# Spreading the last 224 maxima of an attention kernel over 68 units, making the last half's rows by quarters, and giving half chains banks of their own

## The chip, the cores and the metric

The kernel runs on one core of one Trainium2 chip. Time is device microseconds of one execution, lower is better; a time shown is the median of several runs. Profiles are of one execution each. Engines are called PE (TensorE), PEld (its weight loads), DVE (VectorE), ACT (ScalarE), POOL (GpSimd) and SP (SyncE, which issues most DMAs).

## The reference, cut to what matters

For x of 2048 rows and 512 columns two results are mixed by a gate per row. One is the real part of a two-dimensional Fourier transform, written as matrix products; the other is softmax attention with 32 heads of 16 columns.

```python
a = einsum("bsd,ed->bse", x, hid_re);  b = einsum("bsd,ed->bse", x, hid_im)
A = einsum("ts,bse->bte", seq_re, a) - einsum("ts,bse->bte", seq_im, b)
q, k, v = split_heads(x @ wqkv)                      # 32 heads of 16
B = softmax(q @ k.T / 4) @ v                         # each head 2048 x 2048
y = g * A + (1 - g) * (merge(B) @ wo)                # g = sigmoid(x . gate_w)
```

All of it is float32. The kernel gets its precision by splitting each operand into a rounded high part and a low rest, so that a product is three matmuls (high by high, high by low, low by high).

## The kernel before, in words

**Units.** The heads are taken in 16 pairs p, and a pair's keys in 16 tiles of 128 for each half of the queries. A *unit* u is one key tile for one half (hf) of the queries, so a pair has 32 units and the kernel 512 (`UNITS`). The last 16 units (496 to 511) are cut otherwise: blk 0 (496 to 503) is the first quarter of that half's queries, blk 1 (504 to 511) the second, with two key tiles a unit (L711 to L714).

**Scores and maxima.** The two heads of a pair live in the two halves of PE's rows (h = 0 in rows 0 to 63, h = 1 in rows 64 to 127), so that a matmul of one half can run beside a matmul of the other. `scores` (L707) is one matmul of 50 rows and 512 columns and one exponential on ACT (L722). Rows 48 and 49 of the query stack `qs` hold minus the row maximum, as a high and a low part, so that the exponential's argument is already shifted. Those maxima come from `a_tile` (L216): the same product the other way round, 48 rows, followed by a maximum over 512 columns on DVE (L224). A unit needs four maxima matmuls and eight maxima make one row tile `qt`. When all 64 of a pair's half are there, `m_parts` (a maximum over the rest and a negation on DVE, high and low parts on POOL) and `m_rows` (a transpose on DVE, L241, and eight small DMAs into `qs`, L245: four on SP for h = 0, four on POOL for h = 1) are put into the list `deferred`; one entry of it is taken at the end of each segment. Maxima run ahead of scores by 24 units, so that there are none left for the last 24.

**Values.** For two units together `pv` (L747) multiplies the exponentials with the values, in 16 matmuls of 32 columns into one bank; ACT copies the bank out and POOL adds it to a running sum, which goes to DRAM when a pair's half is done. For the last 16 units `pv_last` (L726) keeps one bank through the eight units of a blk, and `LastPair` (L637) brings its result into the output: `copy`, `turn` (pair sums on PE, reciprocal and product on DVE), `back` (a transpose and a split) and `products` (twelve matmuls of 32 rows, four `finish`es and four output DMAs).

**The rest of PE's work** comes from generators of single matmuls (`Chain`): `real` and `dft` (the Fourier part) and `proj` (the output projection by head groups ct = 0 to 3, three matmuls each). `finish` (L589) adds a chain's bank, times 1 - g, to the output row tile on DVE, or on ACT and POOL for tiles in `by_others`. A matmul of a chain may be cut into the two row halves: half 0 beside scores of h = 1, half 1 beside scores of h = 0.

**Order.** All engine queues are written out by hand. A `segment` (L888) walks a pattern: in each slot it issues one chain half (if the slot has one letter) and one score (s) or maximum (a) of the other row half; a slot of two letters issues one for each row half. At "|" it runs the finishes kept back, the plan and the values of two units. A pair of segments serves four units. THIN goes with the hidden transform, FULL (16 slots) with the long one, NINE (12 and 13 slots, nine chain halves each) with the projection of ct 0 to 2: 14 pairs of NINE, for units 432 to 487. The last 24 units run in the loop at L968: scores of both row halves side by side and whole (128 row) matmuls of `proj` between them (`pump`).

**Plan.** `at` (L817) puts functions on a unit, and `run_plan(u)` runs those for units up to u + 1. Around the end: `sums` at 498 and `inverse` at 500 (the denominators of hf 0, ct 3: a DMA in, a reciprocal on DVE, two DMAs out), `last_block` step 0 at 500 (four loads of `o_raw`, L539 and L540), step 1 (a product), step 2 (a split by `parts`, L562 and L563), `load_w15` at 500 (eight DMAs of the weight rows that `products` needs, L634). For hf 1 step 0 at 486 issues twelve such loads.

**Banks.** Of the eight accumulator banks, `psD` (`d_bank`) belongs to the chains. The other seven rotate: `bank` (L381) takes the one that a small model of DVE and ACT expects to be free first, and `o_bank` takes one of them for a chain or a product.

Of the kernel before, what the change touches and what calls it, by code (L numbers as in the profile page):

```python
# [2 lines left out]

# [6 lines left out]
F32 = mybir.dt.float32  # L10
# [21 lines left out]
def mix_kernel(ctx: ExitStack, tc: tile.TileContext, xa_t, xa, wqkv, w_hid, w_seq, wo, gate_w, out):  # L32
# [183 lines left out]
    def a_tile(i, h, ps=None):  # L216
        p, j = divmod(i, 64)
        qt, kb = divmod(j, 4)
        if ps is None:
            ps = turn_of("a")  # L220
        r = slice(64 * h, 64 * h + 48)
        nc.tensor.matmul(ps, qs[p % 2][r, qt * P:(qt + 1) * P], ks[p % 2][r, kb * 512:(kb + 1) * 512],  # L222
                         start=True, stop=True)
        user = nc.vector.tensor_reduce(mx[p % 2][:, h, qt, kb:kb + 1], ps, AX.X, ALU.max)  # L224
# [6 lines left out]
    def m_parts(p, hf):  # L231

        nc.vector.tensor_reduce(nm[hf].rearrange("p (q h) -> p h q", h=2), mx[p % 2][:, :, 8 * hf:8 * hf + 8, :],
                                AX.X, ALU.max, negate=True)
        t = nhl[hf]
        nc.gpsimd.tensor_copy(t[:, 0], nm[hf])
        nc.gpsimd.tensor_tensor(t[:, 1], nm[hf], t[:, 0].bitcast(F32), ALU.subtract)

    def m_rows(p, hf):

        nc.vector.transpose(mt[hf], nhl[hf].rearrange("p v m -> p (v m)").bitcast(F32))  # L241
        for b in range(4):
            for h in range(2):
                rows = qs[p % 2][64 * h + 48:64 * h + 50, hf * 1024:(hf + 1) * 1024].bitcast(F32)
                (nc.sync, nc.gpsimd)[h].dma_start(rows.rearrange("v (q b c) -> v b q c", q=8, b=4)[:, b],  # L245
                                                  mt[hf][32 * b + h:32 * b + 32:2])

    def run_deferred():
        while deferred:
# [149 lines left out]
    def o_bank():  # L399
# [2 lines left out]
        free[i] = now + 10.0  # L402
        return t

    class Chain:


        def __init__(self, take, n):
            self.take, self.left = take, n
            self.begun = False  # L410

        def mm(self, st, mv, half, stop):
            if not self.begun:
                self.ps = self.take()
            r = slice(None) if half is None else slice(64 * half, 64 * half + 64)
            i = nc.tensor.matmul(self.ps, st[r], mv[r], start=not self.begun, stop=stop)  # L416
            self.begun = True
            return i
# [176 lines left out]
            return  # L595
        nc.vector.scalar_tensor_tensor(y, ps, omg[:, t:t + 1], y, op0=ALU.mult, op1=ALU.add)  # L596

    def proj(hf, cts, pools):

        for qt in range(8):  # L600
            t = hf * 8 + qt
            chain = Chain(pools[qt % len(pools)], 3 * len(cts))
            for ct in cts:
                h1, l1 = oh[hf, ct][qt]
                for i, (st, mv) in enumerate(((h1, 0), (h1, 1), (l1, 0))):
                    last = ct == cts[-1] and i == 2
                    yield chain, st, wos[0][:, mv, ct], partial(proj_next, hf, cts, t, chain) if last else None

    def proj_next(hf, cts, t, chain):
        finish(chain.ps, t, yp[t], t in by_others)  # L610
        if hf == 0 and cts[-1] == 3:
            nc.sync.dma_start(out[t * P:(t + 1) * P, :], yp[t])

    def load_yg(hf, ts):
# [22 lines left out]
    class LastPair:  # L637
# [7 lines left out]
            self.o15 = work.tile([P, 2, P], F32R, name="o15", bufs=2)  # L645

        def copy(self, n):
            for c in range(n):
                cols = slice(c * 512 // n, (c + 1) * 512 // n)
                nc.scalar.copy(self.oe[:, cols], self.acc[:, cols])  # L650

        def turn(self):

# [15 lines left out]
        def products(self, others):  # L669

            pss = [o_bank() for _ in range(4)]
            for i, (st, mv) in enumerate(((0, 0), (0, 1), (1, 0))):
                for c in range(4):
                    r = slice(32 * c, 32 * c + 32)
                    nc.tensor.matmul(pss[c], self.o15[r, st], w15[0][r, mv], start=i == 0, stop=i == 2)  # L675
            for c in range(4):
                t = 8 + 4 * self.blk + c
                y = yp.pop(t)
                finish(pss[c], t, y, c in others)
                nc.sync.dma_start(out[t * P:(t + 1) * P, :], y)  # L680

    last_pairs = []

    def last_pair(fill):
        few.append(work.tile([P, 4, D], F32, name="few", tag="pt", bufs=4))
        x = last_pairs[1]
        x.copy(4)
        by_others.update((5, 6))
        pump(fill, 3)
        pump(fill, 3)  # L690
        x.turn()
        x.back()
        drain(fill)
        x.products((0,))
# [82 lines left out]
    def add_sums():  # L777
        while adds:
            adds.pop(0)()
# [26 lines left out]
    def pump(gen, n):  # L806
        for x in take(gen, n, False):
            issue(x, None)
# [8 lines left out]
    def at(u, f, *args):  # L817
        plan.setdefault(u, []).append(partial(f, *args))
# [11 lines left out]

    for p in range(1, NP):
        at(32 * (p - 1) - 1, load_stacks, p)
    one, more = [d_bank], [d_bank, o_bank, o_bank]
# [18 lines left out]

    FULL = "s a s s a a s s a a s a s a a s |"
    THIN = "aS s a s a s s a s a s a a sA |"
    NINE = "aS s a s a sA a a s a s sA |", "aS a s s a sA a s a s s aS sA |"

    def stream(h):

# [26 lines left out]
            for u in us:  # L885
                pv_last(u)

    def segment(pattern, half, ds, stop):  # L888


        nonlocal now
        nonlocal users
        before, users = users, []
        ds, late = iter(ds), []
        for n, slot in enumerate(pattern.split()):
            if slot == "|":
                for f in late:
                    f()
                add_sums()
                run_plan(valued)  # L900
                values()
                continue
            now += 1
            ahead = pattern == FULL and 0 < n < 15
            if ahead:
                score(slot[0], 1 - half)
            if len(slot) == 1:
                x = next(ds, None)
                if x:

                    before = before if x[0].begun else None
                    i = issue(x, half, stop, late)
# [6 lines left out]
            if not ahead:  # L919
                score(slot[0], 1 - half)  # L920
            if len(slot) == 2:
                score(slot[1].lower(), half)
        if deferred:
            deferred.pop(0)()

    def pairs():

        for i in range(NT - 4):
            yield (THIN,) * 2, take(hid, 12)
        for i in range(2 * NT * 3):  # L930
            yield (FULL,) * 2, take(seq, 16)
        for gen, n in ((proj(1, (0, 1, 2), one), 8), (first, 6)):
            for i in range(n):
                yield NINE, take(gen, 9)

    first = proj(0, (0, 1, 2), one)
    run_plan(0)
    gate()

# [17 lines left out]
            segment(patterns[half], half, ds, half == 1)  # L957


    run_plan(valued)  # L960
    for i in range(4):
        score("s", 1)
    third = proj(1, (3,), more)
    last = proj(0, (3,), more)
    whole = {490: (first, 6), 492: (first, 6), 494: (first, 6), 496: (first, 0),
             498: (third, 6), 500: (third, 6), 502: (third, 6), 504: (third, 3), 506: (third, 3),
             508: (last, 6), 510: (last, 9)}
    for u in range(valued + 2, UNITS, 2):  # L968
        add_sums()
        run_plan(u)  # L970
        for i in range(4):
            if i == 2:
                pump(*whole[u])
                if u == 506:
                    last_pairs[0].turn()
                elif u == 508:
                    last_pairs[0].back()
            for h in range(2):
                scores(u + i // 2, i % 2, h)
            for h in range(2):  # L980
                score("a", h)
        if u == 510:
            last_pairs[0].products(())
        values()
        if deferred:
            deferred.pop(0)()
    assert not any(a_left.values())
    values()
    last_pair(last)


# [34 lines left out]
```

## Time and profile before

| what | before |
|---|---|
| median of 3 runs | 1688.01 us (1687.84 to 1688.89) |
| the profiled execution's own time | 1688.01 us |
| its span | 1686.2 us |
| DVE, ACT, POOL busy | 1370.7, 1246.6, 747.8 us |
| maxima on DVE (L224) | 2022 recorded, mean 683 ns |
| exponentials on ACT (L722) | 2048, mean 629 ns |
| clock granted to PE | 0.999 of full speed |

The page's mean of an instruction is from its start to its end. Neighbours on one engine overlap a little, so the distance between two starts is shorter than the mean and is the number to count with. A busy PE says little, since the ends of matmuls are modelled; the distances between starts say more. A few records of matmuls are missing.

### The profile page before, as it was taken

The page shows a single profiled execution, that of the slowest core. Times are in us where ns is not written, and L with a number is a line of the kernel's source. Part 1 is how long each engine was busy: PE and PEld are TensorE (multiplying, and loading weights), DVE is VectorE, ACT ScalarE, POOL GpSimd, SP SyncE. Part 2 cuts the span into 40 slices and gives each one's busy share as a digit, 9 for nine tenths or more (in the row PEclk, how much of TensorE's full clock was granted, in tenths as well). Part 3 has the DMA queues.
Part 4 walks back from the last instruction along what each step waited for, and adds up shares of the span by engine and source line. Part 5 has one row for each costly group of instructions (what it writes and reads, how often), then busy time and mean ns, then how long its engine had stood idle before and what let it go on. Part 6 is the DMA issues. An engine that isn't in the chain of part 4 may idle for free.

```text
span 1686.2 us, 34488 instructions
## 1 busy us (share of the span) xinstructions
PE 1674.4 (99%) x13072; PEld 1016.5 (60%) x13072; DVE 1370.7 (81%) x2283; ACT 1246.6 (74%) x2472; POOL 747.8 (44%) x807
## 2 busy tenths in 40 slices
PE   9999999999999999999999999999999999999998
PEld 7888766655555555555555555555555555565643
DVE  5448688888888888888888888888888888899944
ACT  5212288887777888777777788778777888787896
POOL 0114634554444465444444466445554465322230
PEclk9999999999999999999999999999999999999999
DMA  9963500314141533314155533332241536740114
GB/s 295 340 151 114 174 10 21 45 51 77 44 83 46 102 97 83 70 46 95 45 132 189 103 121 86 86 68 60 70 89 46 112 96 129 263 70 8 33 27 139
DMA packets 82486, 165.15 MB, mean 98 GB/s; under 512 B 19777, under 2 KB 20033, under 8 KB 78481
## 3 DMA queue, kind: packets, MB, share of 16 engines
q1 hardware_dynamic: 77968, 162.56, 37.3%
q8 instruction: 103, 1.69, 0.5%
q0 software_dynamic: 4352, 0.39, 0.3%
q14 instruction: 63, 0.51, 0.1%
HBM read 107.73 MB, written 54.52 MB: 96 GB/s over the span
## 4 chain that ended last, share of the span: by engine, by line
PE 98%; POOL 1%; DMA 0%; issue 0%; DVE 0%; ACT 0%; DVEq 0%; POOLq 0%; ACTq 0%
PE d L416 38%; PE t L757 27%; PE t L222 12%; PE t L721 8%; PE t L315 4%; PE t L89 2%; PE t L90 2%; PE t L88 2%; PE t L333 1%; PE t L738 1%; PE t L416 0%; DMA raw<-wqkv 0%; POOL hl L292 0%; PE t L675 0%; DMA b<-hl 0%
## 5 line engine op out<-in xcount | busy, mean ns | idle before, releaser
L224 DVE TENSOR_REDUCE mx<-t 128x1 f32<-128x512 f32 x2022 | 1253.9, 683 | 197.6 <-PE t L222 153.1
L722 ACT ACTIVATE pt<-t 128x512 f32<-128x512 f32 x2048 | 1035.1, 629 | 9.5 <-PE t L721 9.3
L721 PE MATMUL t<-qs,ks 50*128 50x512 f32 x2048 | 737.5, 411 | 0.6 <-ACT y L432 0.5
L222 PE MATMUL t<-ks,qs 48*128 48x512 f32 x2022 | 689.9, 400 | 0.0
L416 PE MATMUL d<-xab,ch 64*128 64x512 f32 x2016 | 656.9, 400 | 0.0
L757 PE MATMUL t<-pt,vt 128*32 128x512 f32 x3968 | 477.5, 598 | 0.0
L416 PEld LDWEIGHTS d<-xab,ch 64*128 64x128 f32 x2016 | 357.8, 184 | 132.5 <-issue 99.8
L222 PEld LDWEIGHTS t<-ks,qs 48*128 48x128 f32 x2022 | 366.4, 185 | 91.1 <-ACT pt L722 37.4
L721 PEld LDWEIGHTS t<-qs,ks 50*128 50x128 f32 x2048 | 366.8, 185 | 75.3 <-DVE mx L224 34.9
L416 PE MATMUL d<-xab,cl 64*128 64x512 f32 x1008 | 403.8, 401 | 0.0
L772 POOL TENSOR_TENSOR osum<-osum,oe 128x512 f32<-128x512 f32 x217 | 280.1, 1291 | 164.8 <-ACT oe L766 157.4
L766 ACT COPY oe<-t 128x512 f32<-128x512 f32 x217 | 127.7, 589 | 236.1 <-PE t L757 234.3
L757 PEld LDWEIGHTS t<-pt,vt 128*32 128x32 f32 x3968 | 105.0, 109 | 229.6 <-issue 148.7
L371 POOL CAST ch<-craw 128x512 fp32r<-128x512 f32 x126 | 77.4, 615 | 349.8 <-PE t L721 305.2
L416 PEld LDWEIGHTS d<-xab,cl 64*128 64x128 f32 x1008 | 185.7, 184 | 68.2 <-issue 51.1
L372 POOL TENSOR_TENSOR cl<-craw,ch 128x512 fp32r<-128x512 f32 x126 | 162.6, 1290 | 10.2
L245 POOL DMA_DIRECT2D qs<-mt x128 | 72.3, 570 | 81.9 <-DVE mt L241 75.3
L416 PE MATMUL d<-wo_hl,o_hl 64*128 64x512 f32 (+1 forms) x270 | 72.6, 392 | 0.8 <-DVE yp_qs L596 0.8
L416 PE MATMUL d<-wre,xab 64*128 64x512 f32 x288 | 70.4, 389 | 0.0
L416 PEld LDWEIGHTS d<-wre,xab 64*128 64x128 f32 x288 | 52.9, 185 | 3.8 <-DVE mx L224 0.3
L416 PEld LDWEIGHTS d<-wo_hl,o_hl 64*128 64x128 f32 (+1 forms) x270 | 49.5, 185 | 4.8 <-DVE yp_qs L596 1.3
L89 PE MATMUL t<-xab,wh 128*128 128x512 f32 x128 | 49.9, 390 | 0.2 <-DVE xab L85 0.2
(121 smaller groups left out, 893.3 us busy)
## 6 DMA issues: line engine op xcount, KB each, us to landing
craw<-w_seq SPq DMA_DIRECT2D x128, 256.0 KB
qk<-hl SPq DMA_DIRECT2D x32, 512.0 KB
qs<-qk SPq DMA_DIRECT2D x96, 128.0 KB
ks<-qk SPq DMA_DIRECT2D x96, 128.0 KB
b<-hl SPq DMA_DIRECT2D x16, 512.0 KB
xab<-b SPq DMA_DIRECT2D x16, 512.0 KB
o<-osum SPq DMA_DIRECT2D x62, 128.0 KB
oh<-nh SPq DMA_DIRECT2D x12, 512.0 KB
```

Source lines behind the costliest of these rows:

```text
L89: nc.tensor.matmul(ps, sh, ml, start=False, stop=False)
L222: nc.tensor.matmul(ps, qs[p % 2][r, qt * P:(qt + 1) * P], ks[p % 2][r, kb * 512:(kb + 1) * 512], start=True, stop=True)
L224: user = nc.vector.tensor_reduce(mx[p % 2][:, h, qt, kb:kb + 1], ps, AX.X, ALU.max)
L245: (nc.sync, nc.gpsimd)[h].dma_start(rows.rearrange("v (q b c) -> v b q c", q=8, b=4)[:, b], mt[hf][32 * b + h:32 * b + 32:2])
L371: nc.gpsimd.tensor_copy(h1, raw)
L372: nc.gpsimd.tensor_tensor(l1, raw, h1.bitcast(F32), ALU.subtract)
L416: i = nc.tensor.matmul(self.ps, st[r], mv[r], start=not self.begun, stop=stop)
L721: nc.tensor.matmul(ps, ks[p % 2][rr, kt * P:(kt + 1) * P], qs[p % 2][rr, q0:q0 + 512], start=True, stop=True)
L722: return nc.scalar.activation(pts[u][:, 2 * qb + h], ps, AF.Exp, bias=0.0, scale=DH ** -0.5)
L757: nc.tensor.matmul(acc[32 * j:32 * j + 32], vt[:, kt, p, h:h + 32], pt[:, j], start=u == us[0], stop=u == us[-1])
L766: nc.scalar.copy(oe, acc)
L772: nc.gpsimd.tensor_tensor(o, o, oe, ALU.add)
```

## The change

The 14 NINE pairs and the loop become 20 pairs of segments: 8 of FOURTEEN (14 maxima a pair instead of 16), 3 of NINE, then TEN, TWELVE, TEN, TWELVE, TEN with `proj` of ct 0 to 2, and four pairs with `proj` of ct 3 cut into row halves, of which the first is a TEN and the others have no maxima. The last maximum is now in unit 498's segment. For the second half of pair 15 the rows are made by quarters (n = 4) and not by halves (n = 8), and "^" in a pattern takes one entry of `deferred` in mid-segment. In the four last pairs each row half of a chain is a chain of its own in a bank of its own (`held_bank`), with its own finish. `last_block` of hf 1 moves to 486, 489 and 492, that of hf 0 to 500, 503 and 505 with its product on POOL; `load_w15` stays at 500. The wait of a chain's second half is on the first exponential since the chain's last matmul and not on the last one. The copy of the first `LastPair` goes to DVE; `turn` comes three matmuls earlier in `last_pair`; `products` finishes DVE's tiles first and issues the DMA of ACT's tile from ACT's queue.

```diff
-        hf = j // 32
-        a_left[p, hf] = a_left.get((p, hf), 64) - 1
-        if not a_left[p, hf]:
-            deferred.extend((partial(m_parts, p, hf), partial(m_rows, p, hf)))
+        n = 4 if p == NP - 1 and j >= 32 else 8
+        k = qt // n
+        a_left[p, n, k] = a_left.get((p, n, k), 8 * n) - 1
+        if not a_left[p, n, k]:
+            deferred.extend((partial(m_parts, p, n, k), partial(m_rows, p, n, k)))
...
+    def held_bank():
+
+        i, t = bank()
+        free[i] = 1e9
+        last_held[0] = i
+        return t
...
+        if chain.held is not None:
+            free[chain.held] = now + 5
...
+            copy = nc.scalar.copy if self.blk else nc.vector.tensor_copy
...
+            for c in sorted(range(4), key=lambda c: c not in others):
+                t = 8 + 4 * self.blk + c
+                finish(pss[c], t, yp[t], c in others)
             for c in range(4):
                 t = 8 + 4 * self.blk + c
-                y = yp.pop(t)
-                finish(pss[c], t, y, c in others)
-                nc.sync.dma_start(out[t * P:(t + 1) * P, :], y)
+                (nc.scalar if c in others else nc.sync).dma_start(out[t * P:(t + 1) * P, :], yp.pop(t))
...
         pump(fill, 3)
+        x.turn()
         pump(fill, 3)
-        x.turn()
         x.back()
...
+    last = proj(0, (3,), [o_bank, o_bank, o_bank, o_bank, d_bank, o_bank], range(2, 8))
...
-    for step, u in enumerate((486, 490, 494)):
+    for step, u in enumerate((486, 489, 492)):
         at(u, last_block, step, 1, 3, nc.gpsimd)
-    for step, u in enumerate((500, 506, 506)):
-        at(u, last_block, step, 0, 4, nc.vector)
+    for step, u in enumerate((500, 503, 505)):
+        at(u, last_block, step, 0, 4, nc.gpsimd)
     at(500, load_w15)
...
-    NINE = "aS s a s a sA a a s a s sA |", "aS a s s a sA a s a s s aS sA |"
+    NINE = "aS s a s a ^ sA a a s a s sA |", "aS a s s a ^ sA a s a s s aS sA |"
+    FOURTEEN = "s a s a sS ^ a s s a s a aA |", "aS s a a s ^ s a sS s a s a sA |"
+    TWELVE = ("sA a s a s ^ s a s a s s a s |",) * 2
+    TEN = "aA s s a s ^ s s s a a sS |", "a s a sS a ^ s s s s s aA |"
...
-                            i.ins, dict(before).get("s", before[0][1]).ins.name,
+                            i.ins, dict(before[::-1]).get("s", before[0][1]).ins.name,
...
+        for patterns, n in ((FOURTEEN, 8), (NINE, 3), (TEN, 1), (TWELVE, 1), (TEN, 1), (TWELVE, 1), (TEN, 1)):
             for i in range(n):
-                yield NINE, take(gen, 9)
+                yield patterns, take(both_first, 9)
...
+    after = {504: lambda: last_pairs[0].turn(), 506: lambda: last_pairs[0].back(), 510: in_between}
+    for hf, qts in ((1, range(2)), (1, range(2, 5)), (1, range(5, 8)), (0, range(2))):
+        for half in range(2):
+            ds = take(proj(hf, (3,), [held_bank] * (len(qts) - 1) + one, qts, half == 1), 9, False)
+            if valued < UNITS - 12:
+                pattern = TEN[half]
+            else:
+                pattern = "s s s s s s s s |" if len(qts) < 3 else "s s s s d s s s s |"
+                if valued == UNITS - 2:
+                    pattern = "s s s s d d |"
+            segment(pattern, half, ds, True, after.get(valued), False)
     assert not any(a_left.values())
-    values()
     last_pair(last)
```

`in_between` runs `products` of the first `LastPair` and nine whole matmuls of `last` before the values of unit 510.

More of the change, by code (lines that the diff above doesn't have):

```diff
@@ L2 @@
 from functools import partial
+from itertools import chain as chain_of
 import concourse.bass as bass
@@ L596, in finish, with proj @@
         nc.vector.scalar_tensor_tensor(y, ps, omg[:, t:t + 1], y, op0=ALU.mult, op1=ALU.add)
-    def proj(hf, cts, pools):
-        for qt in range(8):
+    def proj(hf, cts, pools, qts=range(8), whole=True):
+        for n, qt in enumerate(qts):
             t = hf * 8 + qt
-            chain = Chain(pools[qt % len(pools)], 3 * len(cts))
+            chain = Chain(pools[n % len(pools)], 3 * len(cts))
             for ct in cts:
@@ L647, in copy @@
         def copy(self, n):
+            copy = nc.scalar.copy if self.blk else nc.vector.tensor_copy
             for c in range(n):
                 cols = slice(c * 512 // n, (c + 1) * 512 // n)
[L650 removed]
+                copy(self.oe[:, cols], self.acc[:, cols])
         def turn(self):
@@ L886, in values, with segment @@
                 pv_last(u)
-    def segment(pattern, half, ds, stop):
+    def segment(pattern, half, ds, stop, between=None, hold=True):
         nonlocal now
@@ L894, in segment @@
         ds, late = iter(ds), []
+        back = late if hold else None
         for n, slot in enumerate(pattern.split()):
@@ L900, in segment @@
                 run_plan(valued)
+                if between:
+                    between()
                 values()
+                continue
+            if slot == "^":
+                if deferred:
+                    deferred.pop(0)()
                 continue
@@ L911, in segment @@
                     before = before if x[0].begun else None
-                    i = issue(x, half, stop, late)
+                    i = issue(x, half, stop, back)
                     users = []
@@ L915, in segment @@
                         tc.add_manual_dep(
-                            i.ins, dict(before).get("s", before[0][1]).ins.name,
+                            i.ins, dict(before[::-1]).get("s", before[0][1]).ins.name,
                             mybir.DependencyInfo(mybir.DependencyClass.Sync, mybir.DependencyReason.DATA))
                         before = None
-            if not ahead:
+            if not ahead and slot != "d":
                 score(slot[0], 1 - half)
@@ L957, in mix_kernel, with in_between @@
             segment(patterns[half], half, ds, half == 1)
[L960 to L983, printed above, removed]
-        values()
-        if deferred:
-            deferred.pop(0)()
+    def in_between():
+        last_pairs[0].products(())
+        pump(last, 9)
+    after = {504: lambda: last_pairs[0].turn(), 506: lambda: last_pairs[0].back(), 510: in_between}
[9 more added lines that the diff above has]
+            segment(pattern, half, ds, True, after.get(valued), False)
     assert not any(a_left.values())
-    values()
     last_pair(last)
```

38 lines of the change are left out of this document (20 added, 18 removed).

## The prediction

> **What bounds the kernel now.** I read the page's span first, then the busy time of three stretches, then the waits of the second, the chain that ended last (for the starts of the value matmuls), and single blocks in the timeline.
>
> ```profile
> span 1686.2 us, 34488 instructions
> ```
> ```profile
> 1301.00:1455.92 154.92, 154.92 (x1280) 90.55 (x1281) 134.07 (x222) 125.69 (x250) 84.56 (x89) 1.00 0.50 124
> 1455.92:1613.61 157.69, 157.69 (x1147) 92.57 (x1145) 145.59 (x243) 126.05 (x252) 42.79 (x46) 1.00 0.25 71
> 1613.61:1670.21 56.60, 55.72 (x347) 24.96 (x346) 20.94 (x32) 51.47 (x103) 12.40 (x13) 1.00 0.27 72
> ```
> ```profile
> PEld t L222 <- DVE mx L224: 26.3, 41, 0.8
> ```
>
> The columns of the stretches are time, then PE, PEld, DVE, ACT, POOL, the clock, DMA share and GB/s. PE reads as busy throughout, but that hides two regimes: in the first stretch (FULL) it runs 1280 matmuls in 154.92 us, in the second (the 14 NINE pairs) 1147 in 157.69. The wait row, of the second stretch, says why: there the weight loads of the maxima waited 26.3 us for DVE. In the third stretch DVE has almost nothing to do. The change moves maxima from the second into the third.
>
> I call two units a *block*: its slots, then 16 value matmuls. A block of FULL on PE:
>
> ```profile
> 1432.66 1.92 PE L757 MATMUL t<-pt,vt 128*32 128x512 f32 x16
> 1434.52 0.50 PE L416 MATMUL d<-xab,ch 64*128 64x512 f32 x1
> ...
> 1438.16 0.40 PE L416 MATMUL d<-xab,ch 64*128 64x512 f32 x1
> 1438.49 1.07 PE L757 MATMUL t<-pt,vt 128*32 128x512 f32 x8
> ```
>
> The values hold PE for 1.86, the sixteen slots start 0.243 apart, and the next values follow the last slot's start by 0.33. So PE alone needs 4.62 us for 11 slots, 4.86 for 12, 5.11 for 13. NINE is slower than that:
>
> ```profile
> 1461.35 1.85 PE t L757 x16
> ...
> 1580.36 1.85 PE t L757 x16
> 1585.72 1.85 PE t L757 x16
> 1591.67 1.85 PE t L757 x16
> ...
> 1608.34 1.85 PE t L757 x16
> 1613.68 2.25 PE t L757 x16
> ...
> 1643.91 1.85 PE t L738 x16
> ...
> 1670.28 3.57 PE t L738 x32
> ```
> ```profile
> 1582.36 0.59 ACT L766 COPY oe<-t 128x512 f32<-128x512 f32 x1 [0.97 <-PE t L757]
> 1582.84 3.54 ACT L722 ACTIVATE pt<-t 128x512 f32<-128x512 f32 x7
> ```
> ```profile
> 1582.68 4.87 DVE L224 TENSOR_REDUCE mx<-t 128x1 f32<-128x512 f32 x8 [0.42 <-PE t L721]
> ```
>
> From value start to value start its two halves take 5.36 and 5.95 (12 and 13 slots): 11.31 a pair. What sets them is the seven rotating banks. Both readers start each block empty (idle 0.97 and 0.42). Counted from the start of the values, maxima give banks back at 2.48+0.60k us, exponentials, behind the copy, at 2.70+0.48k (spacings and starts from the last three rows). The last slot can be issued only when at most seven of the block's scores and maxima are unread. NINE's halves issue 15 and 17 of them, so 8 and 10 must be back: four of each at 4.88, five of each at 5.48. The values follow such a last slot by about 0.43 (the block ending at 1585.72, 4.88 against 5.36, less its own wait): 5.31 and 5.91, against 5.36 and 5.95 measured. The block to 1613.68 (nine exponentials, four maxima) took 5.34, which is 0.2 above PE alone.
>
> **The change part by part.** *FOURTEEN, 8 pairs.* The halves issue 14 and 16, so 7 and 9 must be back: four exponentials and three maxima at 4.62, five and four at 5.10. That gives 5.05 and 5.53, and the second half, with nine exponentials, gets 0.1 more by the block just read. 10.68 x 8 = 85.4 against 90.5 now: this is the gain. *NINE, 3 pairs:* 33.9. *TEN:* 13 issued, 6 back at 4.28, so 4.72; three pairs 28.3. *TWELVE:* PE's 5.11, or 5.15 with its lone slots; two pairs 20.6. The bounds for FOURTEEN are PE alone (9.97 a pair, 5.7 us less in all) and NINE's rate (5 us more).
>
> Values of unit 430 start at 1461.35-5.36 = 1456.0. With 85.4, 33.9, 28.3 and 20.6: unit 494 at 1624.2.
>
> *Splitting the last heads of hf 1 (L562, L563)* falls into block 492, where maxima now stand behind it in DVE's queue:
>
> ```profile
> 1627.44 3.07 POOL L772 TENSOR_TENSOR osum<-osum,oe 128x512 f32<-128x512 f32 x2
> ```
> ```profile
> 1627.71 1.65 DVE L563 TENSOR_TENSOR o_lnh<-o_raw,o_lnh 128x512 fp32r<-128x512 f32 x1
> ```
> ```profile
> 1656.94 1.23 DVE L563 TENSOR_TENSOR o_l<-o_raw,o_l 128x1024 fp32r<-128x1024 f32 x1
> ```
>
> Beside POOL's addition 512 columns took 1.65; alone 1024 took 1.23. At 1.65 for each of the two tiles DVE is over 3 us late and the block about 1 us longer; at 0.6 each it costs nothing. POOL's addition for values 490 ends before values 492 start, so I take nothing and keep 1 us for the range. [...]
>
> *Rows, the added waits.* In DVE's, SP's and POOL's queues they stand where the program puts them:
>
> ```profile
> 1644.71 0.55 DVE L521 RECIPROCAL rc<-rc 128x64 f32<-128x64 f32 x1 [5.57 <-DMA rc<-o]
> ```
> ```profile
> 1661.33 0.75 DVE L596 SCALAR_TENSOR_TENSOR yp<-d,omg,yp 128x512 f32<-128x512 f32 x1 [2.00 <-PE d L416]
> ```
> ```profile
> 1615.91 0.21 DVE L241 STREAM_TRANSPOSE mt<-nhl 128x32 f32<-128x32 f32 x1 [0.60 <-POOL nhl L237]
> ```
> ```profile
> 1620.39 0.59 SPq L540 DMA_DIRECT2D o_raw<-r  x1
> 1621.08 2.75 SPq L245 DMA_DIRECT2D qs<-mt  x4
> ...
> 1649.07 6.18 SPq L634 DMA_DIRECT2D w<-wo  x8
> ```
> ```profile
> qs<-mt POOLq DMA_DIRECT2D x128, 2.0 KB, 1.7
> ```
>
> Pair 15's first half: its last maximum is the last slot of block 474, the first score that reads its rows is slot 7 of block 478, 4.72+3.4 = 8.1 after values 474. The transpose comes behind three maxima (4.3), SP issues for 2.75, the last issue starts 2.1 after the first and lands after 1.7 (POOL's median; SP's is not given): 8.4 with the transpose. Wait 0.3: unit 494 at 1624.5. The last TEN pair copies no sums: 9.4, values 498 at 1633.9, 10 us ahead of 1643.91.
>
> The last quarter: its last maximum is the last slot of block 498. m_parts comes at that block's end, m_rows at the end of block 500, and so behind all that the plan issues at 500: the inverse, four o_raw loads, eight w15 loads. Today's last rows already stood behind such loads: transposed at 1616.1, issued from 1621.08, with no score near. In the changed kernel the reciprocal, too, has to wait: for the three finishes (L596, 0.75) of block 500, of which the last needs slot 9. It starts 0.65 after values 500. From there to the end of the w15 issues it is 1655.25-1644.71 = 10.5, and 3.8 more until the rows have landed: 15.0 after values 500. The first score of unit 504 is slot 6 of block 502, 3.2 after them. PE's queue is in order, so three more scores, values 502 and, behind them, ACT stand too. **11.8 us of PE wait.** Bounds: nothing, if the rows passed the loads; some 15, if the w15 issues slow down beside the scores.
>
> *The last blocks and the tail.*
>
> ```profile
> 1675.28 1.00 PE L656 MATMUL t<-pairsum,oe 128*128 128x64 f32 x8
> ```
> ```profile
> 1677.92 1.02 PE L675 MATMUL t<-w,o 32*128 32x512 f32 x12
> ```
> ```profile
> 1679.68 1.27 POOL L594 TENSOR_TENSOR yp<-yp,few 128x512 f32<-128x512 f32 x1 [1.59 <-ACT few L593]
> ```
> ```profile
> 1680.98 1.82 SPq L680 DMA_DIRECT2D out<-yp  x4
> ```
>
> The accumulator and two half chains hold three banks; nine slots with eight scores then wait for three exponentials (no copy now, third back at 4.03): 4.55 a block. Values 500 come at 1638.5, the rows at 1653.5, and after three slots and 0.43 values 502 at 1654.7. Block 504 is 4.55 and 1.0 for the pair sums (L656), 506 is 4.55 and 0.3 for a transpose (an estimate: under a third of the pair sums), 508 is 4.45: 1669.5. Block 510: values and six slots 3.1, twelve products 1.0 (L675) and 0.5 for their banks (an estimate, most of a finish), nine whole products at a slot's time 2.2, two changes of shape and the way to the values 0.8: 7.7 in all, and 1.85 for the values (half of 3.57): done at 1679.1. The doubled finishes, and the first accumulator's copy, go to a DVE that worked 20.9 us of 56.6 here; without that cover ten finishes are 7 us.
>
> After the last values, 1673.85 today, the span had 12.4 us left. The pair sums now follow three products instead of six (0.7 earlier; ACT's finish in between keeps half of it). SP's four issues began at 1680.98, when POOL's finish was done, and took 1.82; now DVE's three go out as they come, the last at about 1680.7, and POOL's on ACT's queue beside them. Together 1.6 less: 10.8.
>
> **The sum:** 1679.1+10.8 = 1689.9 of span. The profiled execution took 1688.01, which is also the median of the three (1687.84 to 1688.89), so 1.8 lie around its span: **1691.7 us**, 3.7 more than now. Spreading is ahead by 10 at unit 498, the wait takes 11.8, the last blocks lose 3.5 to scores that end later, the tail gives back 1.6.
>
> **The rivals.** *The rows are in time* (faster): SP issues them before PE wants them. For it: I may have counted the way through blocks 500 and 502 short. Against it: today's rows were held 5 us by their queue. 1691.7-11.8 = 1679.9. *Half the wait* (no difference): a w15 issue takes 0.77 here, an o_raw issue 0.59; at that rate, with the reciprocal 4 us earlier because the finishes don't hold it, 6 remain: 1686. *Spreading brings nothing* (the change doesn't do what it says): FOURTEEN runs at NINE's 11.31, its doubled slots bunching the scores. It decides if fewer than nine matmuls are back at 5.5 in the second half; against it, the count met NINE within 0.05. 5 us more: 1697.
>
> **How the numbers follow.** My forecast has 0.58, within 1688.5 to 1695 (FOURTEEN by 0.2 a pair, the wait by 1.5, the end by 1). Rows in time: 0.17. Half the wait: 0.13. No gain: 0.12. A measurement of this kernel can tell about 0.2% from no change: 1684.6 to 1691.4. The forecast lies just above; of its 0.58 I put 0.36 there and 0.22 inside. With 0.12 of the half wait inside, the rest of it and the rows in time below: faster 0.18, same 0.34, slower 0.48. The range goes from 1680, where the rows are in time, to 1698, past the case without a gain.
>
> **What would show it.** Pairs of FOURTEEN at 10.6 between value starts (11.3 would refute the count of banks); values 498 near 1634; SP's last qs issues behind eight w15 ones; PE idle for about 12 us in front of a score (L721's operation) in block 502; value starts otherwise 4.5 to 5.5 apart from 500 to 508; 10.8 after the last values. If there is no idle stretch over 2 us in block 502, the step of the rows is wrong, whatever the total. If it is there and the total is below 1688, the blocks before it gained more than I gave them.

## The result, and the profile after

| | before | after |
|---|---|---|
| median (runs) | 1688.07 us (1687.84 to 1688.89, 6) | 1694.48 us (1693.38 to 1694.97, 6) |
| the profiled execution's own time | 1688.01 us | 1694.88 us |
| its span | 1686.2 us | 1693.1 us |

The changed kernel takes 1.0036 times as long, with a 95% interval of 1.0024 to 1.0049: it is slower by about 6 us. In the changed file the maxima are at L225, the scores at L738, the exponentials at L739, the values at L774 and, for the last 16 units, at L755; the row DMAs are at L248, the loads of w15 at L649.

The page first. The scores' group now shows idle PE, which it did not have before, and it names the DMA of the rows; the list of waits (us in total, times, longest) says that it is one single wait.

```profile
L738 PE MATMUL t<-qs,ks 50*128 50x512 f32 x2048 | 741.8, 410 | 11.3 <-DMA qs<-mt 10.7
```
```profile
PE t L738 <- DMA qs<-mt: 10.5, 1, 10.5
```

The chain that ended last, for the starts of the values:

```profile
1456.07 1.85 PE t L774 x16
...
1531.93 1.85 PE t L774 x16
1537.04 1.91 PE t L774 x16
...
1542.70 1.85 PE t L774 x16
...
1621.55 1.87 PE t L774 x16
...
1626.76 1.85 PE t L774 x16
...
1632.17 1.85 PE t L755 x16
...
1636.88 1.85 PE t L755 x16
...
1657.30 3.57 PE t L755 x16
...
1664.51 1.85 PE t L755 x16
...
1680.28 1.85 PE t L755 x16
```

The eight FOURTEEN pairs, first row to fourth, took 86.6 us, where NINE needed 90.5. Values 498 (the row at 1636.88) come 7.0 us ahead of 1643.91. Values 502 (1657.30) come 4.3 us behind the 1652.96 of the kernel before, and they took 3.57 where the others took 1.85 to 1.91. The row of the kernel before:

```profile
1652.96 1.85 PE t L738 x16
```

The timeline of the changed kernel shows what stands between its values 500, the first row, and the score at which PE waits, the last:

```profile
1641.28 1.92 PE L755 MATMUL t<-pt,vt 128*32 128x512 f32 x16
...
1641.84 0.54 DVE L534 RECIPROCAL rc<-rc 128x64 f32<-128x64 f32 x1
1642.30 0.15 DVE L244 STREAM_TRANSPOSE mt<-nhl 128x32 f32<-128x32 f32 x1
...
1646.18 5.11 SPq L649 DMA_DIRECT2D w<-wo  x8
...
1651.39 2.73 SPq L248 DMA_DIRECT2D qs<-mt  x4
1655.26 0.76 PE L738 MATMUL t<-qs,ks 50*128 50x512 f32 x1 [10.46 <-DMA qs<-mt]
```

The rows are transposed at 1642.30 and issued by SP at 1651.39: for 9.1 us they stand in SP's queue behind the two DMAs of the denominators and the loads of `o_raw` and of w15, and for most of it PE stands with them. The second effect is in the clock. Of a table of stretches (time, length, PE busy, granted clock, DMA share, GB/s) the first and the last row here catch its two changes; a mean of 0.66 is a stretch of 0.2 us with 32% at 1.00 and the rest at 0.50:

```profile
1647.60:1647.80 0.20, 0.00 (x0) 0.66 0.47 82
1647.80:1661.20 13.40, 5.94 (x25) 0.50 0.28 69
1661.20:1661.40 0.20, 0.20 (x4) 0.71 0.00 0
```

The granted clock fell to 0.50 while PE stood, and stayed there for 6 us after work had come back: from 1655.26 to 1661.3 PE ran at half the clock. That is the 3.57.

After the last values, which end at 1682.13, 10.97 us are left, against 12.35 before. The output DMAs of the last tiles now go out on two queues:

```profile
1687.65 1.40 SPq L697 DMA_DIRECT2D out<-yp  x3
1688.63 0.41 ACTq L697 DMA_DIRECT2D out<-yp  x1
```

So the span's 6.9 us are: 7.0 won up to unit 498, 15.3 lost from there to the end of the last values (45.25 us against 29.94), 1.4 won in the tail.

### The profile page after: what moved, and what is told of

It reads as the page before. It is cut to its first block, busy times and chain, and to the rows that moved or that the text cites. A ratio compares the mean times of both kernels' runs of the same rounds, so it can differ in the third digit from the quotient of the medians.

```text
span 1693.1 us, 34606 instructions
## 1 busy us (share of the span) xinstructions
PE 1672.5 (99%) x13120; PEld 1016.5 (60%) x13120; DVE 1375.7 (81%) x2295; ACT 1246.4 (74%) x2471; POOL 751.0 (44%) x814
## 4 chain that ended last, share of the span: by engine, by line
PE 97%; DMA 1%; DVE 1%; POOL 1%; issue 0%; SPq 0%; ACT 0%; DVEq 0%; POOLq 0%; ACTq 0%
PE d L429 39%; PE t L774 27%; PE t L223 12%; PE t L738 7%; PE t L318 4%; PE t L90 2%; PE t L91 2%; PE t L89 2%; PE t L336 1%; PE t L755 1%; PE t L429 1%; DVE mx L225 0%; DMA w<-wo 0%; DMA raw<-wqkv 0%; POOL hl L295 0%
## 5 line engine op out<-in xcount | busy, mean ns | idle before, releaser
L225 DVE TENSOR_REDUCE mx<-t 128x1 f32<-128x512 f32 x2022 | 1254.9, 683 | 211.2 <-PE t L223 171.6
L739 ACT ACTIVATE pt<-t 128x512 f32<-128x512 f32 x2048 | 1034.2, 629 | 23.4 <-PE t L738 12.9
L738 PE MATMUL t<-qs,ks 50*128 50x512 f32 x2048 | 741.8, 410 | 11.3 <-DMA qs<-mt 10.7
L774 PE MATMUL t<-pt,vt 128*32 128x512 f32 x3968 | 477.1, 598 | 0.2
L738 PEld LDWEIGHTS t<-qs,ks 50*128 50x128 f32 x2048 | 371.1, 185 | 78.1 <-DVE mx L225 38.0
L774 PEld LDWEIGHTS t<-pt,vt 128*32 128x32 f32 x3968 | 103.9, 109 | 231.0 <-issue 148.4
L248 POOL DMA_DIRECT2D qs<-mt x132 | 74.1, 567 | 82.2 <-DVE mt L244 77.2
L429 PE MATMUL d<-wo_hl,o_hl 64*128 64x512 f32 x288 | 77.4, 395 | 0.0
L429 PEld LDWEIGHTS d<-wo_hl,o_hl 64*128 64x128 f32 x288 | 52.2, 185 | 14.0 <-DVE yp L609 5.0
```

Source lines behind the costliest of these rows:

```text
L738: nc.tensor.matmul(ps, ks[p % 2][rr, kt * P:(kt + 1) * P], qs[p % 2][rr, q0:q0 + 512], start=True, stop=True)
L739: return nc.scalar.activation(pts[u][:, 2 * qb + h], ps, AF.Exp, bias=0.0, scale=DH ** -0.5)
L774: nc.tensor.matmul(acc[32 * j:32 * j + 32], vt[:, kt, p, h:h + 32], pt[:, j], start=u == us[0], stop=u == us[-1])
```

## The experiments

The theory: the last quarter's rows are late because they stand behind loads in SP's queue, and the idle PE then costs a second time, in the clock. The rivals: the slow stretch after the wait comes from elsewhere (banks, exponentials); behind the row wait the next wait is already there; and the gain of spreading has another cause than the count of banks.

| kernel | median us (runs) | before, same chip | ratio, 95% interval |
|---|---|---|---|
| rows_first | 1685.33 (11) | 1688.22 | 0.9984, 0.9975 to 0.9993 |
| w15_later | 1690.94 (11) | 1688.22 | 1.0015, 1.0006 to 1.0024 |
| fill | 1692.16 (10) | 1688.22 | 1.0023, 1.0013 to 1.0032 |
| six_banks | 1700.49 (1) | 1688.22 | none |
| parts_later | 1683.66 (7) | 1687.97 | 0.9972, 0.9961 to 0.9982 |
| parts_w15 | 1683.68 (9) | 1687.97 | 0.9974, 0.9964 to 0.9984 |
| fill506 | 1688.01 (11) | 1687.97 | 1.0001, 0.9992 to 1.0009 |
| tail | 1687.13 (11) | 1687.97 | 0.9994, 0.9985 to 1.0003 |
| parts_506 | 1681.64 (5) | 1688.57 | 0.9959, 0.9947 to 0.9972 |
| fill_ahead | 1684.46 (10) | 1688.57 | 0.9977, 0.9967 to 0.9986 |

All start from the changed kernel, except tail, which starts from the one before.

### rows_first: the rows ahead of the loads

```diff
-                pattern = "s s s s s s s s |" if len(qts) < 3 else "s s s s d s s s s |"
+                pattern = "s s s s s s s s |" if len(qts) < 3 else "^ s s s s d s s s s |"
```

> The changed kernel with one entry of deferred taken at the start of block 500, so that m_rows of the last quarter is queued before inverse, o_raw and w15 and not behind them. Theory A (the rows stand in SP's queue behind the loads of 500, and PE, idle for 10.5 us, then runs at half clock until about 1661, which costs another 2.5): both go, PE waits under 1 us in block 502, about 1681.5 us, 0.4% faster than before. Theory B (the rows are late whatever their place, because the last maximum itself comes too late; the queue only hides it): the wait stays above 4 us and the time above 1687.

The row wait in block 502 went, and PE kept its clock there, but of the 13.0 us that were expected (1694.5 to 1681.5) only 9.2 came. The timeline of rows_first:

```profile
1639.34 2.73 SPq L248 DMA_DIRECT2D qs<-mt  x4
...
1654.37 0.69 DVE L575 CAST o_l<-o_raw 128x1024 fp32r<-128x1024 f32 x1 [2.92 <-POOL o_raw L587]
...
1656.24 0.20 DVE L674 RECIPROCAL rc<-t 128x8 f32<-128x8 f32 x1
...
1656.98 0.76 PE L738 MATMUL t<-qs,ks 50*128 50x512 f32 x1 [2.23 <-DVE on L676]
...
1659.82 3.64 PE L755 MATMUL t<-pt,vt 128*32 128x512 f32 x16
```

SP issues the rows 12 us sooner. Now DVE is late in block 506: in its queue the split of hf 0 (L575, L576) waits for POOL's product and holds back the reciprocal of `turn`, so the bank of the pair sums comes back late, and a score waits 2.23 us for it. This wait had been in the shadow of the row wait. And again the values after it take twice their time, though PE had stood only 2.23 us.

### w15_later: the rows ahead of the w15 loads alone

```diff
-    at(500, load_w15)
+    at(502, load_w15)
```

> The changed kernel with load_w15 at 502 instead of 500: of what stands in front of the rows only the eight w15 issues (5.1 us) go, the reciprocal and the o_raw loads stay. Theory A: PE waits 10.5-5.1 = 5.4 us. What follows tells two readings of the slow matmuls behind the wait apart. A1 (an idle stretch of a few us costs PE its clock, and it comes back after some us of work): the clock is at 0.50 again for 5 to 6 us, 1689.4. A2 (it takes an idle stretch near 10 us): no half clock, 1687. Theory B: no change, 1694.5.

```profile
1646.37 2.72 SPq L248 DMA_DIRECT2D qs<-mt  x4
```

The rows went out 5.0 us earlier and the score's wait fell from 10.46 to 6.27; the time fell by about 3.5 us, a little less than the wait. So the w15 loads are 4 of the 10.5 us, and the denominators and `o_raw` loads the rest. Of the two readings of the clock A1 held: an idle stretch of 6.27 us cost it too. It fell at 1648.83 and came back at 1655.66, and values 502 took 3.11.

```profile
1648.80:1649.00 0.20, 0.00 (x0) 0.57 1.27 266
...
1655.60:1655.80 0.20, 0.20 (x8) 0.86 0.00 0
```

### fill: the wait kept, PE kept busy in it

```diff
+            if slot == "d" and valued == 502:
+                d, st = d_bank(), wos[0][:, 0, 0][:, :P]
+                for _ in range(40):
+                    nc.tensor.matmul(d, st, wos[0][:, 0, 0], start=True, stop=True)
```

> The changed kernel with 40 more matmuls of 128 rows and 512 columns into the chains' bank in the middle of block 502, whose result nobody reads (work added, nothing left out): 9.4 us of the wait are filled with PE work, and the rows come as late as before. If the half clock is the price of the idle time, the granted clock stays at 1.00, the values of 502 take 1.9 and not 3.6, and the time falls by about 2.5 to 1692. If the matmuls behind the wait are slow for another reason (weights, banks), the time stays at 1694.5 or rises.

```profile
1644.55 9.38 PE L935 MATMUL d<-wo_hl 128*128 128x512 f32 x40
...
1655.99 0.47 PE L738 MATMUL t<-qs,ks 50*128 50x512 f32 x1 [1.42 <-DMA qs<-mt]
...
1657.08 1.92 PE L755 MATMUL t<-pt,vt 128*32 128x512 f32 x16
```

PE does 40 matmuls more, the score comes 0.7 us later, and the kernel is faster: the clock stays at 1.00 and values 502 take 1.92. From the first score to the span's end this kernel needs 1691.0-1655.99 = 35.0 us, the changed one 1693.1-1655.26 = 37.8. The price of the lost clock is 2.8 us.

### six_banks: one rotating bank fewer in the FOURTEEN pairs

```diff
-            i = min(range(7), key=lambda j: free[j])
+            i = min(range(6 if 432 <= valued < 464 else 7), key=lambda j: free[j])
```

> The changed kernel with only six rotating banks for units 432 to 463 (FOURTEEN), seven elsewhere. Theory: the count of banks sets FOURTEEN. Then one more matmul must be back in each block, 8 and 10 as in NINE with seven: 5.3 and 5.95, so about 11.3 a pair instead of 10.8, 4 us in eight pairs, and DVE's work a pair unchanged. Rival: DVE's or PE's own rate sets it (14 maxima take 8.4 us, 25 slots 10): six banks change nothing, 10.8 a pair.

The chain of six_banks, the first row being the start of unit 430:

```profile
1456.36 1.85 PE t L774 x16
...
1537.67 1.85 PE t L774 x16
1543.24 1.85 PE t L774 x16
1549.30 1.85 PE t L774 x16
```

This kernel ran once. The halves now take 5.57 and 6.06, and the eight pairs 92.9 us where the changed kernel took 86.6. No instruction was added for DVE or ACT, so it is the number of banks that sets these blocks. The size was more than expected: the half with few slots, which the count let run at 5.3, lost as much as the other.

### parts_later, parts_w15: the split behind `turn`

```diff
-    for step, u in enumerate((500, 503, 505)):
+    for step, u in enumerate((500, 503)):
...
+    def turn_and_parts():
+        last_pairs[0].turn()
+        last_block(2, 0, 4, nc.gpsimd)
...
-    after = {504: lambda: last_pairs[0].turn(), 506: lambda: last_pairs[0].back(), 510: in_between}
+    after = {504: turn_and_parts, 506: lambda: last_pairs[0].back(), 510: in_between}
```

Both have the edit of rows_first, and parts_w15 that of w15_later too.

> The kernel of rows_first, and of last_block for hf 0 the split (L575, L576) issued behind turn in block 504, no longer ahead of it. In rows_first DVE's first part began at 1654.37 after 2.92 of idleness in front of it, the turn's reciprocal only at 1656.24, and PE stood 2.23 in block 506 and then ran slow: values 506 took 3.64 instead of 1.9. Theory A (the split's place in DVE's queue makes that wait): the wait goes, and with it the slow stretch, 2.2 and about 2.9: 1680.3, which is 1685.3 less 5. Theory B (the turn waits for something else, PE's pair sums or the copy): the wait stays and the time is 1685.

> The kernel of parts_later, and the loads of w15 moved from 500 to 502, behind the o_raw loads of all kinds. Theory A (POOL's product, 10.15 of waiting for o_raw in rows_first, is late because those loads share the DMA engines with w15's): POOL's product begins earlier by 1 us or more; nothing on PE waits for it any more, so 1680 as parts_later, within 0.5. Theory B (w15's later landing delays the products of block 510): up to 3 us more than parts_later.

Theory A was half right. The turn no longer waits, but now the finishes of block 506 stand behind the split, and a score waits for them. First parts_later, then parts_w15:

```profile
1655.94 0.50 PE L738 MATMUL t<-qs,ks 50*128 50x512 f32 x1 [1.40 <-DVE yp L609]
...
1656.87 3.36 PE L755 MATMUL t<-pt,vt 128*32 128x512 f32 x16
```
```profile
1657.07 0.49 PE L738 MATMUL t<-qs,ks 50*128 50x512 f32 x1 [1.36 <-DVE yp L609]
...
1657.98 1.92 PE L755 MATMUL t<-pt,vt 128*32 128x512 f32 x16
```

The edit of parts_w15 turned out to change no queue's order: since the rows are ahead of the loads already, SP issues `o_raw` and then w15 from 500 or from 502 alike. So parts_w15 tells nothing of POOL's late product, but it is a second profile of the same order. The traces of the other kernels say where the product is late. It starts about 5 us after SP's last `o_raw` issue ends in each of them (4.9 in the changed kernel, 5.1 in rows_first) and 5.9 after it in the kernel before; but that issue ends 0.15 us after the start of values 500 in the kernel before and 4.8 after it in rows_first. The loads are issued later, counted in blocks. Whether they also slow each other down was not tested.

The same wait, 1.40 and 1.36 us, cost the clock in the one execution and not in the other. The times show two groups as well. The seven of parts_later are three from 1682.20 to 1682.41 and four from 1683.66 to 1684.21, with nothing between; the mean granted clock is 0.998 in the three longest and 0.999 in the rest. In parts_w15 it is 0.998 in the four longest, 1684.51 to 1684.66, and 0.999 or more in the five from 1682.62 to 1683.68.

### fill506 and fill_ahead: PE kept busy in block 506

```diff
+            if slot == "d" and valued == 506:
+                d, st = d_bank(), wos[0][:, 0, 0][:, :P]
+                for _ in range(9):
+                    nc.tensor.matmul(d, st, wos[0][:, 0, 0], start=True, stop=True)
```

Both have the edit of rows_first. In fill_ahead the first line is `if n == 4 and valued == 506:`.

> The kernel of rows_first, and nine more matmuls of 128 rows and 512 columns, whose result nothing reads, in block 506 ahead of the score at which PE stood 2.23 us. Theory A (the slow values 506 and slots after them in rows_first are the price of the idle stretch in the granted clock): the score comes at the same time, 1657, the clock stays at 1.00, values 506 take 1.9 and the time is 2.9 less than rows_first's, 1682.4, although PE does more work. Theory B (the slow stretch has another cause, the banks or the exponentials): no change, 1685, or more by the work added.

> The kernel of rows_first, and nine more matmuls of 128 rows and 512 columns, whose result nothing reads, in block 506, this time in front of the fourth score and so inside PE's wait of 2.23 us (in fill506 they came out behind the score that waits, and only added work). Theory A (the slow stretch in block 506 is the price of the idle PE): the score comes when it came, values 506 take 1.9 and the clock stays at 1.00, so 1685.3 less what rows_first loses on average to the clock, 1 to 3: 1683.3. Theory B (the slow stretch has another cause): 1685 or up to 2 more for the added work.

fill506 missed its aim: the matmuls came out behind the waiting score, so they filled nothing, ran at half clock in part (0.50 from 1660.28 to 1663.70) and cost 2.7 us. It does not tell the two theories apart. In fill_ahead they stand in front of it:

```profile
1654.40 2.33 PE L935 MATMUL d<-wo_hl 128*128 128x512 f32 x9
...
1656.78 0.46 PE L738 MATMUL t<-qs,ks 50*128 50x512 f32 x1
...
1658.72 1.92 PE L755 MATMUL t<-pt,vt 128*32 128x512 f32 x16
```

The score comes when it came (1656.98 in rows_first), and the clock stays at 1.00. From that score to the span's end it is 1682.6-1656.78 = 25.8 us, in rows_first's profiled execution 1685.6-1656.98 = 28.6. In the medians the gain is smaller and the two intervals overlap, since the profiled rows_first (1687.38) was the slowest of times that reach down to 1683.87; nine of fill_ahead's ten lie between 1683.78 and 1684.78, and the tenth, 1686.88, is not explained. The mean clocks agree: in rows_first 0.999 in the three shortest executions (up to 1684.61) and 0.997 in the three longest (from 1686.69), in fill_ahead 0.999 in all ten. The slow stretch in block 506, too, is the price of an idle PE.

### parts_506: the split behind the finishes of block 506

```diff
-    after = {504: turn_and_parts, 506: lambda: last_pairs[0].back(), 510: in_between}
+    def parts_and_back():
+        last_block(2, 0, 4, nc.gpsimd)
+        last_pairs[0].back()
+
+    after = {504: lambda: last_pairs[0].turn(), 506: parts_and_back, 510: in_between}
```

> The kernel of parts_later, and the split of hf 0 (L575, L576) moved one block further, behind the finishes of block 506. In parts_later those finishes stood behind the split in DVE's queue and a score of block 506 waited 1.40 for them. Theory A (DVE's order makes this wait too, and the wait makes the slow clock of those executions that have it): the wait goes, blocks 504 to 508 are 4.2 to 5.3 each, the clock stays at 1.00 and all times lie close together: 1680.9, which is the faster group of parts_later's times (1682.2 to 1682.4) less 1.4. Theory B (the split is then late for block 508, which multiplies its result): PE stands in block 508 instead, 1 to 2 us, and the time stays at 1682 to 1684.

```profile
1654.08 1.45 DVE L609 SCALAR_TENSOR_TENSOR yp<-t,omg,yp 128x512 f32<-128x512 f32 x2 [2.15 <-PE t L738]
...
1655.95 1.92 PE L755 MATMUL t<-pt,vt 128*32 128x512 f32 x16
1656.26 0.68 DVE L575 CAST o_l<-o_raw 128x1024 fp32r<-128x1024 f32 x1
```

Theory A held, with a time 0.7 us above its 1680.9. The finishes go first, the split begins while PE is at values 506, the waits of the last 60 us list none of PE's, and five times lie within 0.8 us. At 0.9959 of the kernel before this is the fastest kernel of the study, about 7 us less than before and 13 less than the changed kernel, from two edits of order alone: the "^", and the place of the split. The second moves the split further back than either kernel had it: in the kernel before, too, it stood behind values 502 and ahead of `turn`.

### tail: the end of the change alone

```diff
+            for c in sorted(range(4), key=lambda c: c not in others):
+                t = 8 + 4 * self.blk + c
+                finish(pss[c], t, yp[t], c in others)
...
-                nc.sync.dma_start(out[t * P:(t + 1) * P, :], y)
+                (nc.scalar if c in others else nc.sync).dma_start(out[t * P:(t + 1) * P, :], yp.pop(t))
...
-        pump(fill, 3)
         x.turn()
+        pump(fill, 3)
```

> The kernel before, and of the change only its end: products finishes DVE's tiles first and issues the DMAs after, that of ACT's tile from ACT's queue, and turn comes three matmuls earlier. Theory A (the prediction's terms for the tail): after the last values 10.9 us instead of 12.35 are left, so 1688.2 less 1.4, 1686.8. Theory B (the tail of the changed kernel is short for another reason, such as the accumulator's copy or the order of the last block): less than 0.5, 1688.

In its profile 11.15 us are left after the last values (1685.5-1674.35), 1.2 less than before. The median is 0.84 less, between the two theories, and the interval includes no change. The profile shows the shorter tail; the times alone can't tell it from nothing.

## Why the prediction was right or wrong, step by step

| step | predicted | measured |
|---|---|---|
| 8 pairs of FOURTEEN | 85.4 us | 86.6 us |
| values 494 begin | 1624.5 | 1626.8 |
| values 498 begin | 1633.9, 10 ahead | 1636.9, 7.0 ahead |
| values 500 to the first score with the new rows | 15.0 us | 14.0 us |
| PE's wait | 11.8 us | 10.5 us |
| that score to values 504 | 6.75 us | 9.2 us |
| blocks 506, 508, 510 | 4.85, 4.45, 7.7 us | 4.73, 4.22, 6.82 us |
| after the last values | 10.8 us | 10.97 us |
| time | 1691.7 us | 1694.5 us |

**The row wait was right**, in its place, its cause and nearly its size. Its parts: the reciprocal 0.56 after values 500 (0.65 predicted), from there to the end of the w15 issues 9.5 (10.5; a w15 issue took 0.64 and not 0.77), 4.0 more to the score (3.8). rows_first, which issues the rows ahead of all these loads, and w15_later, which moves only the w15 loads behind them, show the cause. The rival of half the wait is refuted by the row itself.

**The step that failed is the score after the wait: "after three slots and 0.43 values 502 at 1654.7", and 5.55 for block 504.** It priced the blocks after an idle stretch of 12 us at the speed of those before it. The runs showed half the granted clock for 6 us and 2.8 us lost; fill kept the rows as late and PE busy, and the clock stayed. The prediction had no term for the clock: in each of the three stretches of the kernel before that it read, the granted clock was 1.00.

**The lead was mis-sized, 7.0 for 10.** Three terms make it up: FOURTEEN 1.2 more than its count; 1.0 more up to unit 494; 0.7 in block 496. six_banks shows that the kind of count was right and its size in the shorter half was not. For the other two the timeline of DVE in the changed kernel says what stood before the maxima, first in block 494, then in block 496:

```profile
1623.72 0.69 DVE L576 TENSOR_TENSOR o_lnh<-o_raw,o_lnh 128x512 fp32r<-128x512 f32 x1
...
1624.33 1.88 DVE L225 TENSOR_REDUCE mx<-t 128x1 f32<-128x512 f32 x3
```
```profile
1630.28 0.74 DVE L609 SCALAR_TENSOR_TENSOR yp<-t,omg,yp 128x512 f32<-128x512 f32 x1
1630.94 0.68 DVE L225 TENSOR_REDUCE mx<-t 128x1 f32<-128x512 f32 x1
1631.54 0.74 DVE L609 SCALAR_TENSOR_TENSOR yp<-d,omg,yp 128x512 f32<-128x512 f32 x1
```

In block 494 four short instructions of the split took 2.2 us of DVE, the subtractions 0.69 each and not 1.65, as the prediction chose; that they cost the block nothing was wrong: it took 5.2 where 4.72 had been forecast. In block 496 the finishes of half chains, for which the prediction named an idle DVE as cover, met the last maxima instead: 5.4. So both causes are read from the order in the timeline; neither was tested by itself. When the two subtractions began, at 1622.65 and 1623.72, POOL stood idle; its next addition began at 1624.28, when the first of them was done and the second nearly so. In the kernel before they took 1.68 beside POOL's DMA issues and 1.65 beside its addition. What made them long there was not tested.

**Block 510 was over-priced** by 0.9 and the way of the rows by 1.0 (14.0 for 15.0), which hides part of the two errors above. The profiled span is 3.2 us longer than the 1689.9 of the prediction: the lead is 3.0 of it and the stretch with the slow clock 2.4 (9.2 for 6.75); the rest goes the other way. That the total came so near is in part luck, since two errors of one sign met several smaller ones of the other.

**The rival "rows in time" was worth what it said, but it was two waits away.** Its 1679.9 is reached to within 1.8 us by parts_506. The changed kernel kept behind the row wait a second one, in DVE's queue, that the prediction did not see. The split of hf 0 did not move ahead of `turn`, although its number in the plan went from 506 to 505: in the kernel before it ended at 1658.2, and the reciprocal of `turn` came behind it:

```profile
1658.75 0.20 DVE L658 RECIPROCAL rc<-t 128x8 f32<-128x8 f32 x1
```

There it had begun 3.3 us after the start of values 502 (1656.22), with the product on DVE and `o_raw` loaded early. In rows_first the plan of 500 runs at the end of block 500, the loads come later, the product is POOL's and takes 2.38 us where DVE's took 1.23, and the split begins 7.9 us after values 502 (1646.45). The prediction gave this path no price. Which of these changes makes how much of the delay was not tested.

## What to carry to other kernels

When work is moved ahead in one engine's queue, write down for each DMA and each vector instruction that the moved path needs what stands in front of it in its own queue: here two lines of order, one on SP and one on DVE, turned 6 us of loss into 7 us of gain. A wait of PE costs itself and can cost the half clock after it (here 2.8 us on top of 10.5); a wait found and removed may uncover the next one, so look at the profile again before the gain is counted. The number of results that may be unread at once (here seven banks) against the rate at which the readers give them back is a good first price for a block: it gave 85.4 us for the eight pairs that took 86.6 (with six banks they took 92.9).

## What the runs showed of the hardware that was not expected

In the profiles shown here the clock's slow stretches ahead of the last values lasted 13.66, 6.83, 6.83 and 3.41 us. From rows of stretches of 0.2 us, in which the share of full clock dates the change to some hundredths: in the changed kernel from 1647.66 to 1661.32 (the rows of 0.66 and 0.71 above), or 13.66. In rows_first, then in parts_later:

```profile
1656.80:1657.00 0.20, 0.02 (x2) 0.78 0.00 0
...
1663.60:1663.80 0.20, 0.20 (x2) 0.65 0.00 0
```
```profile
1657.20:1657.40 0.20, 0.20 (x4) 0.53 0.00 0
...
1660.60:1660.80 0.20, 0.20 (x4) 0.94 0.00 0
```

That is 1656.91 to 1663.74, or 6.83, and 1657.21 to 1660.62, or 3.41. The rows of w15_later above give 6.83 again (1648.83 to 1655.66). The longer ones are about four times and twice the shortest; these are four executions, and what sets the lengths was not tested. In parts_later PE had stood for 1.40 us and worked again for 1.27 (1655.94 to 1657.21) when the clock fell; in fill, after 1.42 us, and in parts_w15, after 1.36 us, it stayed at 1.00. So here a stop of 1.4 us cost the clock in one execution and not in two others. The times of one kernel differ from run to run by 2.0 us in parts_later and in parts_w15 and by 3.5 in rows_first, which have such a wait in their profiles, and by 0.7 in parts_506, which has none. In those three kernels the longest executions go with mean clocks of 0.997 or 0.998, the shortest with 0.999 or more; why the clock falls in one execution and not in the next was not shown.

What stays open: in rows_first PE worked without a pause from 1656.98 on, and the clock came back at 1663.74, 6.8 us later; in parts_later PE worked from 1655.94 on, and the clock came back at 1660.62, 4.7 us later. Nothing in these runs says what brings it back.
